# Routed experts' loop of an attention and mixture-of-experts kernel: one buffer for the next rows becomes two, each filled a step earlier

## Chip, core and metric

The kernel runs on one core of one Trainium2 chip. The metric is the device time of one execution in microseconds (us). The kernel before takes 1048.11 us, the median of 3 runs (1047.6 to 1048.34).

## What is computed

Three layers follow one another: windowed attention over 4 x 768 tokens, a dense three-way max layer, and a routed layer in which each token goes to one of 8 experts. The change touches only the last (E is 8; each expert maps 512 to 1024 and back to 512):

```python
def _moe2_ref(x, w_gate, w_output_gate, w1, w2):
    logits = x @ w_gate
    e_idx = np.argmax(logits, axis=1)
    ...
    for e in range(E):
        mask = e_idx == e
        h = np.maximum(x[mask] @ w1[e], 0.0)
        ye = h @ w2[e]
        out[mask] = gate_w[mask, None] * eom[mask, e, None] * ye
```

x has 3072 rows of 512 float32. Each float32 product is made of three products of high and low parts (`TERMS`), so one weight needs a high and a low copy.

## The kernel before

The tokens are sorted by expert into a DRAM tensor `xs`, one row of 514 values per token: 512 of x and two more, the token's id and its coefficient. After a prologue the loop at L1648 runs over steps. **A step works on two tiles of 128 rows**: tile 0 is the next 128 rows of a list that goes through the experts one after the other ("the list's rows", places in `rowi`), tile 1 the next 128 rows of the first expert ("own rows", places in `owni`). The list's expert has its 1 MB + 1 MB of weights replaced in each step, in 8 pieces of 512 KB; the first expert's weights stay.

A step, as `step` (L1443) writes it, for tile 0 and then tile 1:
- the first layer, 2 x 12 matmuls of 128x512 on TensorE (PE) at L1469, from the transposed rows `xT` of this tile, with ReLU on ScalarE (ACT) at L1475 and the transposes of its result (`h_T`, L1453) a little later;
- `ids` and `x_ids` (L1371): VectorE (DVE) copies the two extra columns of the *next* rows out of their buffer;
- `x_T` (L1355): PE transposes the *next* step's rows of this tile, four 128x128 pieces at L1362, into the PSUM bank `pTx`; ACT (L1364) and DVE (L1366, shown as L185, the line of the helper `sub`) copy the high and the low part into `xT`;
- `load` (L1349): the DMA queue SP reads a place from the list (`value_load`, L1351) and issues the 257 KB load of 128 rows of `xs` (L1353).

Then come the second layers, 2 x 24 matmuls at L1396, scaling on DVE (L1401) and a scatter of the rows by GpSimd (POOL, L1405).

The rows have one buffer, `G["xr"]`, for both tiles. `x_T(0)` reads the list's rows from it; only then can `load("owni", nxt)` refill it with the own rows that `x_T(1)` wants in the same step; after `x_T(1)`, `load("rowi", then)` refills it with the list's rows for the next step. `nxt` is i + 1, `then` is i + 2.

The order of each engine's instructions is set while the program is built: a planner (`Plan`) takes `step` and eight `split` generators, and picks what can start soonest by its own costs. A `split` (L1321) makes the high part of a weight piece on ACT and the low part on DVE, and then issues the load of that piece for the step after (L1335) on SP. So SP's order mixes the eight piece loads of a step with its two row loads, and SP takes them strictly in that order. The prologue (`pro_next`, L1552) loads three times 128 rows into three pieces of the tile `x2r`, and transposes the first two; the third piece stays as `G["xr"]`.

Of the kernel before, what the change touches and what calls it, by code (L numbers as in the profile page):

```python
# [20 lines left out]
P = 128  # L21
# [36 lines left out]
class Plan:  # L58
# [31 lines left out]
    @staticmethod  # L90
    def need(*facts):
        return ("need", facts)

    @staticmethod
    def take(tag):
        return ("take", tag)

    @staticmethod
    def op(eng, cost, r=(), w=(), tail=None, port=True):
        return ("op", eng, cost, r, w, tail, port)  # L100
# [83 lines left out]
def sub(eng, out, in0, in1):  # L184
    eng.tensor_tensor(out=out, in0=in0, in1=in1, op=ALU.subtract)  # L185
# [79 lines left out]
def local_attention_moe_kernel(  # L265
# [17 lines left out]
    nc = tc.nc  # L283
    B, H, S, HD = q.shape
    NT, D = out.shape
# [9 lines left out]
    XW = D + 2  # L295
# [6 lines left out]
    xs = dp.tile([E * REG, XW], F32, name="xs")  # L302
# [12 lines left out]
    with tc.manual_schedule(engines={mybir.EngineType.SP}):  # L315
# [3 lines left out]
        for j, src in enumerate((q, k, v)):  # L319
            t = first_t[j // 2][:, j % 2 * D : (j % 2 + 1) * D]  # L320
            first.append(t.rearrange("p (h d) -> p h d", h=H))
            nc.sync.dma_start(out=first[j], in_=src[0, :, 0:P, :].rearrange("h t d -> t h d"))
            if j:
                _, w, c = wrows[j - 1]
# [7 lines left out]
    for j in range(2):  # L332
        nc.vector.scalar_tensor_tensor(
            out=gl[:, j : j + 1], in0=nf[:, 2 * j + 1 : 2 * j + 2], scalar=4294967296.0,
# [23 lines left out]
    op, need, take, give, state = plan.op, plan.need, plan.take, plan.give, plan.state  # L358
    PE, DVE, ACT, POOL, DMA = "PE", "DVE", "ACT", "POOL", "DMA"
# [5 lines left out]
    def pe(columns, products=1):  # L365
        return products * (columns / 2400.0 + 0.013)

    def act(n):
        return 0.17 + n * 0.00085

    def dve(n):
        return 0.155 + n * 0.00104
# [4 lines left out]
    def psum(cost, r=(), w=()):  # L377

        return op(DVE, cost, r, w, port=False)

    def dma(nbytes, r=(), w=(), held=False, rate=DMA_RATE):
        return op(DMA, 0.5, r, w, tail=(0.06 + nbytes / rate, held))
# [228 lines left out]
    G = {}  # L611
# [485 lines left out]
    NL = MAXT - 2  # L1097
# [242 lines left out]
    T = {}  # L1340
    def fresh():
        ES_AT.written = LISTS_AT.written = 0.0
        for name in ("xr", "xT", "xT0", "xT1", "hr0", "hr1", "h00", "h01", "h10", "h11", "yc", "yd", "nx", "bx", "cid", "did"):
            T[name] = Buf(None)
        for name in ("pTx", "pT0", "pT1", "pH0", "pH1", "pc", "pd"):
            T[name] = Buf(None, True)
        T["W"] = [[Buf(None), Buf(None)] for _ in range(2)]

    def load(name, idx):  # L1349
        yield op(DMA, 0.6, [LISTS_AT])  # L1350
        r = nc.sync.value_load(G[name][0:1, idx], min_val=0, max_val=E * REG - P)  # L1351
        yield dma(P * XW * 4, w=[T["xr"]])
        nc.sync.dma_start(out=G["xr"], in_=xs[bass.ds(r, P), :])  # L1353

    def x_T(half):  # L1355

        xr, xb = G["xr"], T[f"xT{half}"]
        pTx = G["pTx"].rearrange("p (a b) -> p a b", b=P)
        xh, xl = [t[:, :, half * P : (half + 1) * P] for t in G["xT"]]
        for d in range(KD):  # L1360
            yield op(PE, 0.109, [T["xr"]], [T["pTx"]])
            nc.tensor.transpose(pTx[:, d, :], xr[:, d * P : (d + 1) * P], ident)  # L1362
        yield op(ACT, act(D), [T["pTx"]], [xb])
        nc.scalar.copy(out=xh, in_=pTx)  # L1364
        yield psum(dve(D), [T["pTx"], xb], [xb])
        sub(nc.vector, xl, pTx, xh.bitcast(F32))  # L1366

    def x_ids(dst):

        yield op(DVE, 0.16, [T["xr"]], [T[dst]])  # L1370
        nc.vector.tensor_copy(out=G[dst], in_=G["xr"][:, D:])  # L1371

    def ids(src, dst):
        yield op(DVE, 0.16, [T[src]], [T[dst + "id"]])
        nc.vector.tensor_copy(out=G[dst + "id"], in_=G[src][:, 0:1])
        yield op(DVE, 0.16, [T[src]], [T[dst + "id"]])
        nc.vector.tensor_copy(out=G[dst + "co"], in_=G[src][:, 1:2])
# [8 lines left out]
    def h_place(n, own, f):  # L1386

        if f == 0:
            return G["hh"][n][:, 0:4, own * P : (own + 1) * P]
        t = G["hh"][n][:, 4:6] if own else G["hx"][n]  # L1390
        return t.rearrange("p a (b c) -> p (a b) c", b=2)
# [48 lines left out]
    GROUPS = (0, 2, 3, 1)  # L1440
    FIRST_Y = (0, 1, 4, 5, 6, 7, 2, 3)

    def step(nxt, then, pl):  # L1443

        late = []

        def h_T():
            own, f = late.pop()
            hb = T[f"h{own}{f}"]
            pT = G["pg"][f].rearrange("p (a b) -> p a b", b=P)  # L1450
            for d in range(4):
                yield op(PE, 0.109, [T[f"hr{f}"]], [T[f"pT{f}"]])
                nc.tensor.transpose(pT[:, d, :], hm_t[f][:, d * P : (d + 1) * P], ident)  # L1453
            hh, hl = [h_place(m, own, f) for m in range(2)]
            yield op(ACT, act(512), [T[f"pT{f}"]], [hb])
            nc.scalar.copy(out=hh, in_=pT)
            yield psum(dve(512), [T[f"pT{f}"], hb], [hb])
            sub(nc.vector, hl, pT, hh.bitcast(F32))

        for own in range(2):  # L1460
            W, Wb = G["W"][1 - own], T["W"][1 - own]
            xT = [t[:, :, own * P : (own + 1) * P] for t in G["xT"]]
            for f in range(2):
                b = slice(f * 512, (f + 1) * 512)
                ph = G["pg"][2 + f]
                for d in range(KD):
                    yield op(PE, pe(512, 3), [T[f"xT{own}"], Wb[0]], [T[f"pH{f}"]])
                    for m, (A_, B_) in enumerate(TERMS):
                        nc.tensor.matmul(ph, lhsT=xT[A_][:, d, :], rhs=W[d][B_][:, b], start=(d + m == 0), stop=(d == KD - 1 and m == 2))  # L1469
                    if f == 1:  # L1470
                        pl.state("first", own, d)
                    if d == 2 and late:
                        yield from h_T()
                yield op(ACT, act(512), [T[f"pH{f}"]], [T[f"hr{f}"]])
                nc.scalar.activation(out=hm_t[f], in_=ph, func=AF.Relu)  # L1475
                late.append((own, f))
            yield from ids("nb"[own] + "x", "dc"[own])
            yield from x_ids("nb"[own] + "x")
            yield from x_T(own)
            yield from load(*(("rowi", then) if own else ("owni", nxt)))  # L1480
        for own in range(2):
            n = "dc"[own]
            W, Wb = G["W"][1 - own], T["W"][1 - own]
            for f in range(8):
                yield op(PE, pe(512, 3), [T[f"h{own}{f // 4}"], Wb[1]], [T["p" + n]])
                y_step(lambda m: h_place(m, own, f // 4)[:, f % 4, :], f, W, G["p" + n], f == 7)
                if f % 2:
                    pl.state("second", own, f // 2)
                if late and f == 1:
                    yield from h_T()  # L1490
            yield from y_out(n, T["p" + n], T["y" + n], T[n + "id"], True)
# [59 lines left out]

    def pro_next():  # L1552
        yield need(("lists",), ("p1",), *[("routed", n) for n in range(NTILE)])
        xbs = []
        for name, n in (("rowi", 0), ("owni", 0), ("rowi", 1)):
            xb = yield take("x2r")
            T["xr"], G["xr"] = xb, xb.t
            yield from load(name, bass.ds(n, 1))
            xbs.append(xb)
        bank = yield take("bank")  # L1560
        T["pTx"], G["pTx"] = bank, bank.t
        for t in range(2):
            T["xr"], G["xr"] = xbs[t], xbs[t].t
            yield from x_ids("nb"[t] + "x")
            T[f"xT{t}"] = T["xT"]
            yield from x_T(t)
        T["xr"], G["xr"] = xbs[2], xbs[2].t


    ET = mybir.EngineType  # L1570
# [34 lines left out]
    with tc.manual_schedule(engines={ET.PE, ET.Activation, ET.DVE, ET.Pool, ET.SP}):  # L1605
# [7 lines left out]
        for t, fill in ((rel, MASK), (rel0, 0.0)):  # L1613
            nc.gpsimd.affine_select(
                out=t, in_=rel0, pattern=[[-1, NG]], compare_op=ALU.is_ge, fill=fill, base=0, channel_multiplier=1
# [3 lines left out]
        for j in range(2):  # L1619
# [4 lines left out]
            out=reli[:, NG:], in_=reli[:, NG:], pattern=band, compare_op=ALU.is_ge, fill=MASK, base=NPREV, channel_multiplier=1  # L1624
# [21 lines left out]

    trip = nc.values_load(G["trip"][0:1, 0:1], min_val=0, max_val=NL - 2, skip_runtime_bounds_check_because="counts of tokens per expert")
    with tc.For_i(0, trip, 1, iteration_sync="reg_based") as i:  # L1648
        nxt = nc.s_assert_within(i + 1, 0, NL - 2, skip_runtime_bounds_check_because="places in the lists")
        then = nc.s_assert_within(i + 2, 0, NL - 1, skip_runtime_bounds_check_because="places in the lists")  # L1650
        fresh()
        pl = Plan(LATE_T)
        for s in staged:
            s.free = s.written = s.last = 0.0
            s.by = s.last_by = None
        pl.add(step(bass.ds(nxt, 1), bass.ds(then, 1), pl), (0,))
        for d in range(NPC):
            pl.add(split(pl, 2 * NPC + d, [("first", 0, d) if d < KD else ("second", 0, d - KD)], bass.ds(then, 1)), (2, d), HOLD_T)
        with tc.manual_schedule(engines=ALL):
            pl.run()  # L1660
# [31 lines left out]
```

## Time and profile before

| | |
|---|---|
| median of 3 runs | 1048.11 us |
| the profiled execution's own time | 1046.29 us |
| its span, first to last instruction | 1044.6 us |
| mean granted TensorE clock | 0.975 of full speed |
| PE busy | 961.0 us, 92% |
| DVE busy | 650.5 us, 62% |
| ACT busy | 498.6 us, 48% |
| POOL busy | 179.1 us, 17% |
| the loop of 13 steps, first matmul to last | 680.57 to 1035.51 us of the span, 354.94 us |

The span is the time between the first and the last instruction; 1.69 us of the profiled execution lie around it. Busy shares are of the span. The line numbers in the rows are those of the code above. A row of the timeline merges instructions of one kind: its start, its length, the engine, the line, the operation, output and input, how many, and in brackets the idle time of the engine ahead of it with what ended it.

### The profile page before, as it was taken

The numbers are of one execution on the slowest core, as the hardware profiler recorded it, in microseconds if no ns is written. First come the engines' busy times: TensorE is split into PE (matmuls) and PEld (weight loads), VectorE is DVE, ScalarE is ACT, GpSimd is POOL, SyncE is SP. The second block draws the span as 40 slices with busy tenths as digits, with TensorE's granted clock in tenths as the row PEclk, the third lists the DMA queues.
The fourth block names the chain that finished last, engine by engine and source line by source line (L and its number), as shares of the span: only waits on it lengthen the run. The fifth ranks groups of instructions, "written<-read, shape, count | busy, mean of one in ns | idle before, by whom it ended". The sixth has DMA issues, their size and how long they took to land. (4 is left out here: it accounts for less than half of the span.)

```text
span 1044.6 us, 22019 instructions
## 1 busy us (share of the span) xinstructions
PE 961.0 (92%) x7768; PEld 847.0 (81%) x7768; DVE 650.5 (62%) x1680; ACT 498.6 (48%) x1070; POOL 179.1 (17%) x246
## 2 busy tenths in 40 slices
PE   2469999999999999999999999989999999999995
PEld 2358988999989898999989998877777777777774
DVE  5998887777776667642652346655555555555553
ACT  4776665656545665422232133155554444445542
POOL 5444331213022221110110001100000000000000
PEclk9769999999999999999999999999999999999998
DMA  8998795676756677450340023376555555555555
GB/s 248 274 186 217 192 218 146 151 155 145 162 129 139 154 144 142 95 163 31 104 140 21 21 76 107 100 267 189 200 185 184 194 193 189 179 192 179 194 191 170
DMA packets 225603, 166.19 MB, mean 159 GB/s; under 512 B 181676, under 2 KB 181676, under 8 KB 225520
## 3 DMA queue, kind: packets, MB, share of 16 engines
q1 hardware_dynamic: 221360, 152.48, 54.3%
q0 software_dynamic: 4160, 12.62, 3.3%
q8 instruction: 50, 0.82, 0.3%
q14 instruction: 33, 0.27, 0.1%
HBM read 116.16 MB, written 24.78 MB: 135 GB/s over the span
## 5 line engine op out<-in xcount | busy, mean ns | idle before, releaser
L914 PE MATMUL bank<-xT,w 128*128 128x256 f32 x2592 | 336.0, 287 | 3.6 <-DVE xT L185 3.6
L914 PEld LDWEIGHTS bank<-xT,w 128*128 128x128 f32 x2592 | 318.6, 192 | 6.5 <-DVE xT L185 4.2
L185 DVE TENSOR_TENSOR w<-ws_more,w 128x1024 fp32r<-128x1024 f32 x79 | 95.5, 1222 | 71.6 <-ACT w L1321 66.0
L781 ACT ACTIVATE sp<-sp,mn 128x232 f32<-128x232 f32 (+1 forms) x192 | 90.5, 472 | 52.1 <-DVE mn L774 43.2
L986 PE MATMUL bank<-w,hh 128*128 128x512 f32 x432 | 110.4, 400 | 0.0
L944 DVE TENSOR_TENSOR hm<-hm,bank 128x512 f32<-128x512 f32 x72 | 49.3, 684 | 65.9 <-PE bank L914 64.4
L986 PEld LDWEIGHTS bank<-w,hh 128*128 128x128 f32 x432 | 77.5, 188 | 14.6
L1321 ACT CAST w<-ws_more 128x1024 fp32r<-128x1024 f32 x79 | 80.3, 1049 | 18.7 <-PE bank L1453 9.8
L1469 PE MATMUL bank<-wp,xT 128*128 128x512 f32 x312 | 82.2, 405 | 0.0
L831 PE MATMUL bank<-va,aT 128*128 128x64 bf16 x1760 | 64.8, 198 | 15.0 <-DMA aT<-nat 13.6
L1469 PE MATMUL bank<-w,xT 128*128 128x512 f32 x312 | 76.4, 394 | 1.6 <-ACTq L1648 1.6
L1475 ACT ACTIVATE hm<-bank 128x512 f32<-128x512 f32 x52 | 31.1, 597 | 95.5 <-PE bank L1469 95.5
L831 PEld LDWEIGHTS <-aT 128*128 128x128 f16 x1760 | 59.1, 101 | 20.1 <-DMA aT<-nat 15.6
L1396 PE MATMUL bank<-w,hh 128*128 128x512 f32 x246 | 68.1, 414 | 0.0
L1469 PEld LDWEIGHTS bank<-w,xT 128*128 128x128 f32 x312 | 57.6, 188 | 12.9 <-ACT xT L1364 1.8
L774 DVE CUSTOM_DVE_ANT_0 sp<-bank,bias 128x232 f32<-128x232 f32 x160 | 59.1, 389 | 10.1 <-PE bank L750 10.1
L1469 PEld LDWEIGHTS bank<-wp,xT 128*128 128x128 f32 x312 | 55.8, 189 | 10.4
L1396 PE MATMUL bank<-wp,hh 128*128 128x512 f32 x258 | 62.6, 395 | 0.0
L1086 POOL DMA_INDIRECT xs<-x2r,di x24 | 24.6, 1025 | 208.7 <-DVE x2s L185 121.4
L1396 PEld LDWEIGHTS bank<-wp,hh 128*128 128x128 f32 x258 | 48.4, 188 | 11.6
L185 POOL TENSOR_TENSOR seen<-x,dco 128x1 f32<-128x1 f32 x14 | 3.5, 252 | 303.7 <-DVE x L1401 293.6
L657 POOL TENSOR_TENSOR qkn<-qkn,va 128x512 f32<-128x512 f32 x23 | 29.3, 1272 | 139.7 <-ACT va L655 117.1
(238 smaller groups left out, 1535.3 us busy)
## 6 DMA issues: line engine op xcount, KB each, us to landing
ws_more<-in_moe_w_dram SPq DMA_DIRECT2D x85, 512.0 KB, 4.4
bias<-in_moe_w_dram SPq DMA_DIRECT2D x22, 512.0 KB, 4.6
ws<-in_moe_w_dram SPq DMA_DIRECT2D x21, 512.0 KB
x2r<-xs SPq DMA_DIRECT2D x29, 257.0 KB, 3.2
x<-xd SPq DMA_DIRECT2D x28, 256.0 KB
xd<-xo SPq DMA_DIRECT2D x24, 256.0 KB
qkn<-in_q_dram SPq DMA_DIRECT2D x23, 256.0 KB
qkn<-in_k_dram SPq DMA_DIRECT2D x23, 256.0 KB
```

What stands on the lines that cost most here:

```text
L185: eng.tensor_tensor(out=out, in0=in0, in1=in1, op=ALU.subtract)
L657: nc.gpsimd.tensor_tensor(out=vf, in0=vf, in1=va.t[:, 0, :], op=ALU.subtract)
L774: nc.vector.tensor_tensor_reduce(out=o[:, g:], in0=x[:, g:], in1=bias[:, pr, n0 + g :], scale=scale, scalar=low, op0=ALU.add, op1=ALU.min, ...
L781: nc.scalar.activation(out=o, in_=o, func=AF.Exp, scale=-1.0, bias=mn[:, h : h + 1], accum_out=sm[:, h : h + 1])
L831: nc.tensor.matmul(po[:, h, :], lhsT=a, rhs=V, start=(n == 0), stop=(n == len(terms) - 1))
L914: nc.tensor.matmul(pj[:, f2, :], lhsT=W[:, d, fs], rhs=X[:, d, :], start=(d + n == 0), stop=(d == KD - 1 and n == 2))
L944: nc.vector.tensor_max(out=hv, in0=hv, in1=pj)
L986: nc.tensor.matmul(bank.t, lhsT=X[:, f, t * P : (t + 1) * P], rhs=W[:, f, :], start=(f + n == 0), stop=(f == KF - 1 and n == 2))
L1321: (nc.scalar.copy if eng == ACT else nc.vector.tensor_copy)(out=h, in_=s.t)
L1396: nc.tensor.matmul(py, lhsT=at(A_), rhs=w, start=(f + m == 0), stop=(last and m == 2))
L1469: nc.tensor.matmul(ph, lhsT=xT[A_][:, d, :], rhs=W[d][B_][:, b], start=(d + m == 0), stop=(d == KD - 1 and m == 2))
L1475: nc.scalar.activation(out=hm_t[f], in_=ph, func=AF.Relu)
```

## The change

There are two row buffers, `G["xr"][0]` for the list's rows and `G["xr"][1]` for the own rows. In the loop each is refilled right behind the `x_T` that reads it, with the rows of the step after the next one: both loads now use `then` (i + 2). The prologue loads the first rows of both, and after each of its two `x_T` calls the rows at place 1. `x_ids` takes the tile's number, and `nxt` is gone.

```diff
--- before.py
+++ after.py
@@ -1340,35 +1340,36 @@
     T = {}
     def fresh():
         ES_AT.written = LISTS_AT.written = 0.0
-        for name in ("xr", "xT", "xT0", "xT1", "hr0", "hr1", "h00", "h01", "h10", "h11", "yc", "yd", "nx", "bx", "cid", "did"):
+        for name in ("xr0", "xr1", "xT", "xT0", "xT1", "hr0", "hr1", "h00", "h01", "h10", "h11", "yc", "yd", "nx", "bx", "cid", "did"):
             T[name] = Buf(None)
         for name in ("pTx", "pT0", "pT1", "pH0", "pH1", "pc", "pd"):
             T[name] = Buf(None, True)
         T["W"] = [[Buf(None), Buf(None)] for _ in range(2)]
 
-    def load(name, idx):
+    def load(name, idx, own):
         yield op(DMA, 0.6, [LISTS_AT])
         r = nc.sync.value_load(G[name][0:1, idx], min_val=0, max_val=E * REG - P)
-        yield dma(P * XW * 4, w=[T["xr"]])
-        nc.sync.dma_start(out=G["xr"], in_=xs[bass.ds(r, P), :])
+        yield dma(P * XW * 4, w=[T[f"xr{own}"]])
+        nc.sync.dma_start(out=G["xr"][own], in_=xs[bass.ds(r, P), :])
 
     def x_T(half):
 
-        xr, xb = G["xr"], T[f"xT{half}"]
+        xr, xb = G["xr"][half], T[f"xT{half}"]
         pTx = G["pTx"].rearrange("p (a b) -> p a b", b=P)
         xh, xl = [t[:, :, half * P : (half + 1) * P] for t in G["xT"]]
         for d in range(KD):
-            yield op(PE, 0.109, [T["xr"]], [T["pTx"]])
+            yield op(PE, 0.109, [T[f"xr{half}"]], [T["pTx"]])
             nc.tensor.transpose(pTx[:, d, :], xr[:, d * P : (d + 1) * P], ident)
         yield op(ACT, act(D), [T["pTx"]], [xb])
         nc.scalar.copy(out=xh, in_=pTx)
         yield psum(dve(D), [T["pTx"], xb], [xb])
         sub(nc.vector, xl, pTx, xh.bitcast(F32))
 
-    def x_ids(dst):
-
-        yield op(DVE, 0.16, [T["xr"]], [T[dst]])
-        nc.vector.tensor_copy(out=G[dst], in_=G["xr"][:, D:])
+    def x_ids(own):
+
+        n = "nb"[own] + "x"
+        yield op(DVE, 0.16, [T[f"xr{own}"]], [T[n]])
+        nc.vector.tensor_copy(out=G[n], in_=G["xr"][own][:, D:])
 
     def ids(src, dst):
         yield op(DVE, 0.16, [T[src]], [T[dst + "id"]])
@@ -1440,7 +1441,7 @@
     GROUPS = (0, 2, 3, 1)
     FIRST_Y = (0, 1, 4, 5, 6, 7, 2, 3)
 
-    def step(nxt, then, pl):
+    def step(then, pl):
 
         late = []
 
@@ -1475,9 +1476,9 @@
                 nc.scalar.activation(out=hm_t[f], in_=ph, func=AF.Relu)
                 late.append((own, f))
             yield from ids("nb"[own] + "x", "dc"[own])
-            yield from x_ids("nb"[own] + "x")
+            yield from x_ids(own)
             yield from x_T(own)
-            yield from load(*(("rowi", then) if own else ("owni", nxt)))
+            yield from load(("rowi", "owni")[own], then, own)
         for own in range(2):
             n = "dc"[own]
             W, Wb = G["W"][1 - own], T["W"][1 - own]
@@ -1551,20 +1552,18 @@
 
     def pro_next():
         yield need(("lists",), ("p1",), *[("routed", n) for n in range(NTILE)])
-        xbs = []
-        for name, n in (("rowi", 0), ("owni", 0), ("rowi", 1)):
-            xb = yield take("x2r")
-            T["xr"], G["xr"] = xb, xb.t
-            yield from load(name, bass.ds(n, 1))
-            xbs.append(xb)
+        G["xr"] = []
+        for own in range(2):
+            T[f"xr{own}"] = xb = yield take("x2r")
+            G["xr"].append(xb.t)
+            yield from load(("rowi", "owni")[own], bass.ds(0, 1), own)
         bank = yield take("bank")
         T["pTx"], G["pTx"] = bank, bank.t
-        for t in range(2):
-            T["xr"], G["xr"] = xbs[t], xbs[t].t
-            yield from x_ids("nb"[t] + "x")
-            T[f"xT{t}"] = T["xT"]
-            yield from x_T(t)
-        T["xr"], G["xr"] = xbs[2], xbs[2].t
+        for own in range(2):
+            T[f"xT{own}"] = T["xT"]
+            yield from x_ids(own)
+            yield from x_T(own)
+            yield from load(("rowi", "owni")[own], bass.ds(1, 1), own)
 
 
     ET = mybir.EngineType
@@ -1646,14 +1645,13 @@
 
     trip = nc.values_load(G["trip"][0:1, 0:1], min_val=0, max_val=NL - 2, skip_runtime_bounds_check_because="counts of tokens per expert")
     with tc.For_i(0, trip, 1, iteration_sync="reg_based") as i:
-        nxt = nc.s_assert_within(i + 1, 0, NL - 2, skip_runtime_bounds_check_because="places in the lists")
         then = nc.s_assert_within(i + 2, 0, NL - 1, skip_runtime_bounds_check_because="places in the lists")
         fresh()
         pl = Plan(LATE_T)
         for s in staged:
             s.free = s.written = s.last = 0.0
             s.by = s.last_by = None
-        pl.add(step(bass.ds(nxt, 1), bass.ds(then, 1), pl), (0,))
+        pl.add(step(bass.ds(then, 1), pl), (0,))
         for d in range(NPC):
             pl.add(split(pl, 2 * NPC + d, [("first", 0, d) if d < KD else ("second", 0, d - KD)], bass.ds(then, 1)), (2, d), HOLD_T)
         with tc.manual_schedule(engines=ALL):
```

What the planner makes of it on the engines follows at three places. `L1351 TENSOR_LOAD` is the reading of the place, `L1353 DMA x2r<-xs` the load of 128 rows, `L1335 DMA` and `L1308 DMA` loads of weight pieces (in the loop and in the prologue), `ISA` and `REGISTER_ALU` bookkeeping. A wait in brackets names the semaphore: an engine's, or that of a DMA slot (`DMAHW0` to `DMAHW7`, given to the DMAs of the loop's body in turn, so the fourth DMA has `DMAHW3`, the sixth `DMAHW5`); the ending `_own` marks those that the loop's body counts, the others are from the prologue.

SP in the loop, from behind the third piece load of a step, before:

```order
L1351 TENSOR_LOAD owni
L1351 ISA x2
L1353 ISA
L1353 DMA x2r<-xs 128x514 [waits DMAHW5_I-9128_own,DMAHW3_I-9128_own,PE_I-9128_own]
L1335 ISA
L1335 DMA ws_more<-in_moe_w_dram 128x1024 [waits DVE_I-9128_own,DMAHW4_I-9128_own,Activation_I-9128_own,DMAHW4_49]
L1351 ISA
L1351 TENSOR_LOAD rowi
L1351 ISA x2
L1353 ISA
L1353 DMA x2r<-xs 128x514 [waits DMAHW3_I-9128_own,DVE_I-9128_own,PE_I-9128_own]
```

and now:

```order
L1351 TENSOR_LOAD rowi
L1351 ISA x2
L1353 ISA
L1353 DMA x2r<-xs 128x514 [waits DMAHW3_I-9138_own,PE_I-9138_own,DMAHW4_49]
L1335 ISA
L1335 DMA ws_more<-in_moe_w_dram 128x1024 [waits DVE_I-9138_own,DMAHW4_I-9138_own,Activation_I-9138_own,DMAHW3_49]
L1351 ISA
L1351 TENSOR_LOAD owni
L1351 ISA x2
L1353 ISA
L1353 DMA x2r<-xs 128x514 [waits DVE_I-9138_own,DMAHW5_I-9138_own,PE_I-9138_own,DMAHW7_49]
```

The places of the two row loads among the piece loads are the same. The fourth DMA of the body was the own rows' load and is now the list rows', the sixth the other way round.

PE in the loop, around `x_T(1)` at the end of the first layers, before:

```order
L1453 MATMUL bank_525<-ident,hm_546 128x128 [waits DVE_I-9128_own,Activation_I-9128_own]
L1453 MATMUL bank_525<-ident,hm_546 128x128 x3
L1469 MATMUL bank_530<-wp_6756,xT_717 128x512 x2
L1469 MATMUL bank_530<-wp_6756,xT_718 128x512
L1362 REGISTER_ALU
L1362 MATMUL bank_524<-ident,x2r 128x128 [waits DMAHW3_I-9128_own,DVE_I-9128_own]
L1362 MATMUL bank_524<-ident,x2r 128x128 x3
L1396 MATMUL bank_527<-w_676,hh_1869 128x512
```

and now:

```order
L1454 MATMUL bank_525<-ident,hm_546 128x128 [waits DVE_I-9138_own,Activation_I-9138_own]
L1454 MATMUL bank_525<-ident,hm_546 128x128 x3
L1470 MATMUL bank_530<-wp_6756,xT_717 128x512 x2
L1470 MATMUL bank_530<-wp_6756,xT_718 128x512
L1362 REGISTER_ALU
L1362 MATMUL bank_524<-ident,x2r 128x128 [waits DMAHW5_I-9138_own,DVE_I-9138_own,DMAHW7_49]
L1362 MATMUL bank_524<-ident,x2r 128x128 x3
L1397 MATMUL bank_527<-w_676,hh_1869 128x512
```

The order is the same. The transposes waited for the fourth DMA of the body, which SP issues ahead of them in the same step; now they wait for the sixth, which SP issues behind them, so it is the one of the step before.

SP in the prologue, before (a piece load follows at once, eight in a row):

```order
L1351 TENSOR_LOAD owni [waits DVE_49]
L1351 ISA x2
L1353 ISA
L1353 DMA x2r<-xs 128x514 [waits DVE_49,DMASW1_49,PE_49,DMASW7_49,Activation_49,Pool_49]
L1351 TENSOR_LOAD rowi
L1351 ISA x2
L1353 ISA
L1353 DMA x2r<-xs 128x514 [waits DVE_49,DMASW2_49,PE_49,DMASW5_49,Activation_49,Pool_49]
L1305 TENSOR_LOAD esi [waits DVE_49]
L1305 ISA x2
L1308 ISA
L1308 DMA ws_more<-in_moe_w_dram 128x1024
```

and now, behind the first four piece loads:

```order
L1351 TENSOR_LOAD rowi
L1351 ISA x2
L1353 ISA
L1353 DMA x2r<-xs 128x514 [waits DMAHW4_49,DMAHW6_49,DVE_49,PE_49]
L1308 ISA
L1308 DMA ws_more<-in_moe_w_dram 128x2x512 [waits DMAHW5_49]
L1308 ISA
L1308 DMA ws_6757<-in_moe_w_dram 128x2x512 [waits Activation_49]
L1351 TENSOR_LOAD owni
L1351 ISA x2
L1353 ISA
L1353 DMA x2r<-xs 128x514 [waits DMAHW7_49,DVE_49,PE_49]
```

One row load that stood ahead of all eight piece loads now stands behind four of them, and another that was the first step's stands behind six; each waits for PE and DVE to have read the buffer.

## Rows read from the trace of the kernel before

**Rows 1.** Chain of work that ended last, shares of the span by line.

```profile
PE bank L1396 14%; PE bank L1469 11%; DMA x2r<-xs 5%; PE bank L1453 2%; PE bank L1362 1%; POOLq L1687 0%; DVE x L1401 0%; POOL seen L185 0%; POOLq L1648 0%; POOLq L1405 0%; POOLq L185 0%
```

**Rows 2.** Waits of PE in the loop: us in total, times, longest us.

```profile
PE bank L1362 <- DMA x2r<-xs: 23.7, 13, 2.5
```

**Rows 3.** Timeline of PE, third step, around `x_T(0)` and `x_T(1)`.

```profile
739.44 0.94 PE L1469 MATMUL bank<-w,xT 128*128 128x512 f32 x3
740.23 0.60 PE L1362 MATMUL bank<-ident,x2r 128*128 128x128 f32 x4
740.58 2.35 PE L1469 MATMUL bank<-wp,xT 128*128 128x512 f32 x9
...
746.53 0.94 PE L1469 MATMUL bank<-wp,xT 128*128 128x512 f32 x3
748.98 0.63 PE L1362 MATMUL bank<-ident,x2r 128*128 128x128 f32 x4 [1.50 <-DMA x2r<-xs]
749.36 1.64 PE L1396 MATMUL bank<-w,hh 128*128 128x512 f32 x6
750.84 0.60 PE L1453 MATMUL bank<-ident,hm 128*128 128x128 f32 x4
```

**Rows 4.** Timeline of the other engines, third step.

```profile
743.63 0.68 DVE L185 TENSOR_TENSOR xT<-bank,xT 128x512 fp32r<-128x512 f32 x1
745.09 0.33 SPq L1353 DMA_DIRECT2D x2r<-xs  x1
747.57 0.60 ACT L1475 ACTIVATE hm<-bank 128x512 f32<-128x512 f32 x1 [0.17 <-PE bank L1469]
748.10 0.14 DVE L1377 COPY cco<-bx 128x1 f32<-128x1 f32 x1
758.19 0.37 SPq L1335 DMA_DIRECT2D ws_more<-in_moe_w_dram  x1
```

**Rows 5.** Steps: us, busy of PE, PEld, DVE, ACT, POOL (instructions), PEclk, DMA share, GB/s.

```profile
680.57:707.46 26.89, 25.46 (x121) 20.50 (x122) 14.56 (x21) 13.59 (x18) 1.20 (x2) 1.00 0.78 269
734.48:761.20 26.72, 25.22 (x122) 20.23 (x121) 15.32 (x22) 13.59 (x18) 2.37 (x4) 1.00 0.58 199
815.97:845.24 29.27, 26.80 (x121) 21.43 (x121) 15.40 (x22) 13.59 (x18) 2.38 (x4) 0.94 0.53 166
872.00:900.95 28.95, 26.79 (x121) 21.43 (x121) 15.40 (x22) 13.58 (x18) 2.38 (x4) 0.94 0.54 176
```

**Rows 6.** Timeline of PE, the longest waits of `x_T(1)`: fifth, sixth, eighth step.

```profile
803.75 0.63 PE L1362 MATMUL bank<-ident,x2r 128*128 128x128 f32 x4 [2.49 <-DMA x2r<-xs]
831.43 0.63 PE L1362 MATMUL bank<-ident,x2r 128*128 128x128 f32 x4 [2.47 <-DMA x2r<-xs]
887.16 0.90 PE L1362 MATMUL bank<-ident,x2r 128*128 128x128 f32 x4 [2.16 <-DMA x2r<-xs]
```

**Rows 7.** Short windows behind these waits and a long one earlier, columns as in rows 5.

```profile
803.00:805.00 2.00, 1.25 (x8) 1.14 (x9) 0.17 (x1) 0.54 (x1) 0.00 (x0) 1.00 0.24 95
833.00:835.00 2.00, 2.00 (x8) 1.63 (x7) 0.52 (x1) 0.89 (x1) 0.00 (x0) 0.50 0.51 132
889.00:891.00 2.00, 2.00 (x9) 1.51 (x8) 0.52 (x1) 0.21 (x1) 0.00 (x0) 0.55 0.43 132
180.00:320.00 140.00, 140.00 (x1642) 129.11 (x1641) 104.46 (x353) 81.60 (x238) 29.07 (x36) 1.00 0.69 147
```

**Rows 8.** Loads of rows in the loop: us from issue to landing.

```profile
DMA to landing us min/median/max: 2.6/3.2/4.7
```

**Rows 9.** Timeline of the prologue's end and the first step: SP, DVE and PE.

```profile
669.75 2.99 SPq L1353 DMA_DIRECT2D x2r<-xs  x3
673.54 2.99 SPq L1308 DMA_DIRECT2D ws_more<-in_moe_w_dram  x5
677.23 0.16 DVE L1371 COPY nx<-x2r 128x2 f32<-128x2 f32 x1
686.57 0.60 PE L1362 MATMUL bank<-ident,x2r 128*128 128x128 f32 x4
```

## The prediction

> **What bounds the kernel now.** I read the chain of waits first [rows 1]: what ended last is work of PE, with one other entry of weight, the row loads x2r<-xs, at 5% of the span (some 52 us). That is more than a change of the load can win, since the chain counts each load from its issue, while PE still works for most of it. The waits of PE in the loop say what it really costs [rows 2]: from the first step's start to the last one's end PE waits for one thing only, 13 times, once a step, for 23.7 us in all, and it is the transposes of x_T at L1362.
>
> The timeline of the third step shows which of the two x_T it is [rows 3]. x_T(0) starts right behind three matmuls, without a wait. x_T(1) ends a wait of 1.50 us. The engine rows beside it show why [rows 4]: the own rows' load is issued at 745.09, because the one buffer had to be read by x_T(0) first and because SP was still at the weight pieces; PE is done with its first layer near 747.4; the load takes 2.6 to 4.7 us to land [rows 8].
>
> The table of steps says that nothing else holds PE there [rows 5]: the third step lasts 26.72 us with PE busy for 25.22, and the difference is just the 1.50 us of the wait. ACT with 13.59 and DVE with 15.32 are far from the step's length, the DMA share is near 0.6. So each step is PE's work plus one load that comes too late.
>
> **The change part by part.** *The wait of x_T(1) goes*: x_T(1) now waits for a load that was issued a step earlier. In the loop the own rows' load is issued once x_T(1) and the copy bx are through. That copy stands on DVE behind the one that starts at 748.10 [rows 4], so the issue comes near 749; the rows are wanted a step of some 25 us later, near 772. The landing takes 4.7 us at most [rows 8], so about 18 us of cover are left. The list rows' load, issued near 745 as the own rows' was, is wanted by the next step's x_T(0), some 20 us later. Gain: 13 waits, 23.7 us [rows 2].
>
> *PE's pipeline closes over the gap.* From the start of the three matmuls ahead of it to the start of the matmuls behind it, x_T(0) takes 740.58 - 739.44 = 1.14 us, x_T(1) takes 749.36 - 746.53 = 2.83 us [rows 3]. The difference is 1.69 us, and the wait is 1.50 of it; the other 0.19 us is the end of one group that otherwise overlaps the next. 13 x 0.19 = 2.5 us, so 26.2 us with the waits.
>
> *The clock.* Two steps, the sixth and the eighth, are longer than their wait explains: 29.27 - 2.47 = 26.80 and 28.95 - 2.16 = 26.79 us, against 26.72 - 1.50 = 25.22 [rows 3, 5, 6]. In both the granted clock is 0.50 to 0.55, so the lower of the two levels, 1.2 GHz, in a window right behind the wait, and PE had just stood idle for over 2 us; the fifth step's 2.49 us wait is followed by full clock [rows 6, 7]. Each fall costs 1.58 us, two of them 3.15. Without idle time in the step I take them as gone, since earlier PE is busy without a break for 140 us at a clock of 1.00 [rows 7]. Sum: 26.2 + 3.15 = 29.35 us.
>
> The Trainium skill bears on this in "TensorE: Matmul & The Clock Gate", Part 1: the gate follows PE's activity in a free-running window that does not start with the work, so that it is a matter of phase which gap costs. That agrees with a fall behind 2.16 us and none behind 2.49; it would also make the number of falls differ from run to run, and one more fall in the runs than in the profiled execution would be 1.58 of the 1.82 us between them. By that, all falls gone, the median would end near the profiled sum. The same page, under "HAM oscillation", gives as its abstract rule that only longer idle gaps than these reopen the throttle; by that rule the two falls have some other cause and stay. That is a rival below.
>
> *What takes the wait's place in a step.* With x_T(1) 1.69 us earlier, three things stand next. The bank pTx is free when DVE ends the low part of x_T(0), 743.63 + 0.68 = 744.31, 3 us ahead of x_T(1). The rows have landed. The last h_T of the step, at 750.84 now, will want to start at 749.15, and needs ACT's ReLU at 747.57 + 0.60 = 748.17 [rows 3, 4]: 0.98 us of slack. All other work of ACT and DVE in the second layers starts from PE's matmuls and moves with them. The weight pieces are loaded a step ahead: the last is issued at 758.19 [rows 4] and split a step later, so a step that is 2 us shorter leaves over 15 us of cover. Cost 0.
>
> *SP in the loop* has the same order; only the names of the two row loads are exchanged. The first still stands behind the third piece load and needs x_T(0); the second still needs x_T(1). Cost 0.
>
> *The prologue* trades one row load ahead of the eight piece loads for two among them. The first of these must wait for the copy nx, 677.23 + 0.16 = 677.39, and its rows are wanted at 686.57 [rows 9]. It has four piece loads of 512 KB ahead of it. The three row loads of before start 1.33 us apart (2.99 us for three, less one's own 0.33, over two), so without the third the pieces start near 673.54 - 1.33 = 672.2; 2.1 MB and 0.26 MB at the 269 GB/s of the first step [rows 5] take 8.8 us, so landing is near 682 and, by the longest landing after issue, 677.4 + 4.7 = 682.1: 4 us of cover. At worst it shares the DMA engines with all eight pieces and both row loads, 4.7 MB in 17.5 us, and lands at 689.7: 3.1 us late, once. Bounds 0 and 3.1; I take 0, as the loads start in order. The loop's first load of SP comes at some 682, and the first row it has to serve is a step away. The extra rows of DVE and SP are single register instructions: 0.
>
> **The sum.** The profiled execution took 1046.29 us, 1.82 less than the median of the runs. 1046.29 - 29.35 = 1016.9. From the median, 1048.11 - 29.35 = 1018.8, and a third fall that goes too would make it 1017.2. I take **1017.5 us**, nearer the sum that counts a third fall.
>
> **The rivals.**
> - *The falls of the clock stay* (the rule named above, as a mechanism: something other than the idle time lowers it for some 3 us, twice or three times in the loop). Then only the 26.2 us come: 1046.29 - 26.2 = 1020.1, from the median 1021.9. For it: 2.49 us of idle time without a fall. Against it: both falls begin right behind a wait, and among the longest three [rows 6, 7]. Chance 0.08.
> - *ACT takes the wait's place*: the last h_T of each step waits for ReLU, which has only 0.98 us of slack. If ACT runs another 0.6 us copy ahead of it and PE arrives earlier than I think, 0.5 us stay in each step: 13 x 0.5 = 6.5, so 1024.0. Against it: the ReLU stands ahead of that copy on ACT now. Chance 0.05.
> - *The change does not do what it says*: both buffers are pieces of one tile, and a wait on the whole tile would tie x_T(1) to the load of this step, issued even later. Then 1048. Against it: the wait names the sixth DMA alone. Chance 0.02.
> - *Slower, by the clock*: 325 us of PE work without a pause could lower the granted clock for long stretches. At half clock each us gives half a us of work, so the loss passes the gain of 29.35 us from 59 us at half clock on; 100 us at it would give 1017.5 + 50 = 1067.5. Against it: 140 us of PE without a pause at 1.00 [rows 7]. Chance 0.02.
>
> **How the numbers follow.** The forecast has 0.83. The range goes from 1014 (some 3 us below the lowest sum, for a pipeline gain of 0.4 instead of 0.19 us a step) to 1022.5 (the clock's rival from the median, or the prologue's 3.1 us on the higher sum); it leaves out the last three rivals, 0.09. A measurement can tell about 0.2%, 2.1 us, from no change. Faster: forecast, clock's rival and ACT's rival, 0.96. Same: 0.02. Slower: 0.02.
>
> **What would show it.** In the profile after: no wait of L1362 for x2r<-xs in the loop, each x_T(1) some 0.8 us behind the start of the three matmuls ahead of it, steps of 25.0 us each with granted clock 1.00, and a loop of about 325.6 us (354.94 in the table of the profile before, less 29.35). PE's busy time would fall by 3 us at most. Wrong would be a step with full clock above 25.3 us (then a new wait stands in it, and its releaser names the rival), steps with a clock of 0.94, or a first step that stands out by a wait of x_T(0) (the prologue's loads).

## The result and the profile after

The changed kernel takes **1017.0 us** (median of 4 runs, 1016.35 to 1018.69) against 1048.05 us of the kernel before (4 runs). The ratio is 0.9707, 95% interval 0.969 to 0.9723. The profiled execution took 1016.92 us, 29.37 less than that of before.

The head of the page and its chain of work that ended last (by engine, by line):

```profile
span 1015.4 us, 22036 instructions
PE 955.8 (94%) x7768; PEld 845.3 (83%) x7768; DVE 651.2 (64%) x1680; ACT 497.0 (49%) x1070; POOL 178.8 (18%) x246
...
PE 32%; POOLq 0%; issue 0%; DVE 0%; POOL 0%
PE bank L1470 14%; PE bank L1397 14%; PE bank L1454 2%; PE bank L1362 1%; POOLq L1685 0%; DVE x L1402 0%; POOL seen L185 0%; POOLq L1647 0%; POOLq L1406 0%; POOLq L185 0%
```

The row loads have left the chain [rows 1]. (Most lines of the step have moved down by one, so the first layer is L1470 and the second L1397; x_T is still L1362.) The waits of PE from the second transposes of the prologue to the last step (us in total, times, longest us):

```profile
PE bank L1470 <- ACTq L1647: 1.5, 1, 1.5
PE bank L1362 <- DVE xT L185: 1.4, 1, 1.4
```

Both stand before the first matmul of the loop. The 13 waits for x2r<-xs [rows 2] are gone, and none has come in their place. The third step on PE, with the same pieces as [rows 3]:

```profile
736.21 0.94 PE L1470 MATMUL bank<-w,xT 128*128 128x512 f32 x3
736.99 0.60 PE L1362 MATMUL bank<-ident,x2r 128*128 128x128 f32 x4
737.34 2.35 PE L1470 MATMUL bank<-wp,xT 128*128 128x512 f32 x9
...
743.30 0.94 PE L1470 MATMUL bank<-wp,xT 128*128 128x512 f32 x3
744.07 0.60 PE L1362 MATMUL bank<-ident,x2r 128*128 128x128 f32 x4
744.43 1.63 PE L1397 MATMUL bank<-w,hh 128*128 128x512 f32 x6
745.90 0.60 PE L1454 MATMUL bank<-ident,hm 128*128 128x128 f32 x4
```

From the three matmuls ahead of x_T(1) to the matmuls behind it now takes 744.43 - 743.30 = 1.13 us, as for x_T(0); it was 2.83 [rows 3]. SP issues the two row loads of the same step at these times:

```profile
741.86 0.33 SPq L1353 DMA_DIRECT2D x2r<-xs  x1
...
745.48 0.33 SPq L1353 DMA_DIRECT2D x2r<-xs  x1
```

The first is the list rows' load, wanted by the next step's x_T(0) at 761.99; the second the own rows', wanted at 769.08. They land as slowly as before, which no longer matters:

```profile
DMA to landing us min/median/max: 2.8/3.7/4.8
```

The steps (us, busy time and number of instructions of PE, PEld, DVE, ACT, POOL, granted clock, DMA share, GB/s):

```profile
679.28:706.08 26.80, 26.80 (x120) 21.55 (x121) 14.57 (x21) 13.48 (x18) 2.21 (x3) 0.94 0.81 269
706.08:731.09 25.01, 25.01 (x122) 20.28 (x120) 15.33 (x22) 13.48 (x18) 2.39 (x4) 1.00 0.65 209
...
981.15:1006.16 25.01, 25.01 (x121) 20.10 (x119) 15.32 (x22) 13.48 (x18) 2.38 (x4) 1.00 0.64 206
sum 326.88, PE 326.88 PEld 264.81 DVE 198.45 ACT 175.27 POOL 30.82; mean PE 25.14 PEld 20.37 DVE 15.27 ACT 13.48 POOL 2.37
```

and the last matmuls of the loop:

```profile
1004.79 1.53 PE L1397 MATMUL bank<-w,hh 128*128 128x512 f32 x6
```

Twelve of the 13 steps take 25.00 or 25.01 us at full clock, and PE is busy for all of it. From the first matmul to the end of the last, as in the table of the kernel before, the loop takes 1004.79 + 1.53 - 679.28 = 327.04 us (the sum of the rows stops 0.16 us ahead of that end), against 354.94: 27.90 less. It also begins 1.29 us earlier, 679.28 against 680.57; the loads ahead of it already went out 1.19 us earlier (668.56 against 669.75 [rows 9]), so that came from the work before the changed code. It differs between executions: in the changed kernel's second profile, shown below, the loop begins at 680.73. What follows the loop takes 9.1 us, as before. 27.90 + 1.29 = 29.2 us of span.

### The profile page after: what moved, and what is told of

It reads as the page before. It is cut to its first block, busy times and chain, and to the rows that moved or that the text cites. A ratio compares the mean times of both kernels' runs of the same rounds, so it can differ in the third digit from the quotient of the medians.

```text
span 1015.4 us, 22036 instructions
## 1 busy us (share of the span) xinstructions
PE 955.8 (94%) x7768; PEld 845.3 (83%) x7768; DVE 651.2 (64%) x1680; ACT 497.0 (49%) x1070; POOL 178.8 (18%) x246
## 5 line engine op out<-in xcount | busy, mean ns | idle before, releaser
L986 PE MATMUL bank<-w,hh 128*128 128x512 f32 x432 | 110.4, 400 | 0.0
L1470 PE MATMUL bank<-wp,xT 128*128 128x512 f32 x312 | 82.1, 405 | 0.0
L1470 PE MATMUL bank<-w,xT 128*128 128x512 f32 x312 | 78.1, 400 | 1.5 <-ACTq L1647 1.5
L1470 PEld LDWEIGHTS bank<-w,xT 128*128 128x128 f32 x312 | 58.7, 192 | 13.4 <-ACT xT L1364 1.7
L1397 PE MATMUL bank<-w,hh 128*128 128x512 f32 x246 | 65.5, 401 | 0.0
L1470 PEld LDWEIGHTS bank<-wp,xT 128*128 128x128 f32 x312 | 55.7, 189 | 10.5
L1397 PE MATMUL bank<-wp,hh 128*128 128x512 f32 x258 | 62.6, 395 | 0.0
L1397 PEld LDWEIGHTS bank<-wp,hh 128*128 128x128 f32 x258 | 48.4, 188 | 11.6
L185 DVE TENSOR_TENSOR nat<-sp,nat 128x928 f16<-128x928 f32 (+1 forms) x45 | 52.0, 1155 | 1.1 <-ACT nat L795 0.3
```

Of the source, the lines that this page charges most:

```text
L986: nc.tensor.matmul(bank.t, lhsT=X[:, f, t * P : (t + 1) * P], rhs=W[:, f, :], start=(f + n == 0), stop=(f == KF - 1 and n == 2))
L1397: nc.tensor.matmul(py, lhsT=at(A_), rhs=w, start=(f + m == 0), stop=(last and m == 2))
```

## The experiments

The theory: each step lost the time by which the own rows landed after PE wanted them, and now and then a fall of TensorE's clock behind that idle time. Three questions were open: whether the buffer or the time of issue did it, whether the clock really falls because of the wait, and what holds the kernel now. The first three runs shared one chip, on which the kernel before took 1043.32 us (13 runs, 1037.62 to 1050.51); the last three shared another, with 1047.74 us (9 runs, 1043.06 to 1048.97).

### The second buffer alone

From the changed kernel, with the loads at their old places (the rows of places i + 1 and i + 2, as before):

```diff
-            yield from load(("rowi", "owni")[own], then, own)
+            yield from load(*(("rowi", then, 0) if own else ("owni", nxt, 1)))
```

The step takes `nxt` (i + 1) again for this. In the prologue only the list's rows are loaded a second time.

> Two row buffers, but both loads at their old places: the own rows' load still fetches the next step's rows, and the planner still puts it behind the third piece load of the step. My theory: SP's order, not the buffer, set when the own rows' load went out (x_T(0) is through 4 us before it). So the load goes out as late as before, x_T(1) waits 1.4 to 2.5 us in each of 13 steps, some 23.7 us in all, and the time is that of the kernel before: 1046 to 1049.5 us. Rival: the buffer held the load back; then it goes out 2 us or more earlier, the waits fall below 0.5 us, and the time is 1017 to 1024 us.

Measured: 1048.27 us (10 runs, 1044.38 to 1051.21), ratio to the kernel before 1.0031 (1.0003 to 1.0059). Waits of PE in the loop, then SP and PE in the third step, and that step (columns as above):

```profile
PE bank L1362 <- DMA x2r<-xs: 22.6, 13, 2.7
PE bank L1362 <- issue: 1.7, 1, 1.7
```

```profile
742.75 3.80 SPq L1335 DMA_DIRECT2D ws_more<-in_moe_w_dram  x3
747.55 0.33 SPq L1353 DMA_DIRECT2D x2r<-xs  x1
```

```profile
742.61 0.60 PE L1362 MATMUL bank<-ident,x2r 128*128 128x128 f32 x4
...
752.55 1.09 PE L1362 MATMUL bank<-ident,x2r 128*128 128x128 f32 x4 [2.69 <-DMA x2r<-xs]
```

```profile
736.71:767.44 30.73, 28.04 (x122) 22.46 (x121) 15.40 (x22) 13.59 (x18) 2.38 (x4) 0.89 0.49 170
```

The buffer of the own rows had been free for most of a step, and still the load went out at 747.55, 4.3 us after x_T(0) was through, right behind the third piece load. That piece load waits for VectorE's low part of the piece, and SP waits with it, as the waits of SP in the loop of this run say:

```profile
SPq L1335 <- DVE w L185: 221.5, 88, 8.8
```

So a second buffer by itself gives nothing: the planner's place of the load in SP's order set the time. Whether the 0.3% by which it came out slower is real stays open; the runs of both kernels scatter by 7 to 13 us on this chip. Part of it may be the wait of 1.7 us, which x_T(0) has in the first step and which the kernel before has not. The profile names no releaser for it. The row load that this x_T(0) reads went out at 679.77, behind the eight piece loads of the prologue, and ahead of them before [rows 9], so it is the likely cause. The clock fell in 3 of the 13 steps, behind waits of 2.69, 2.42 and 2.42 us; the profiled execution was the slowest of the ten (1051.21 us).

### One buffer, with the load issued earlier

From the kernel before; the first three piece loads of a step wait, in the plan, until the own rows' load has its place on SP (the upper lines are in `step`, the lower ones in `split`):

```diff
             yield from load(*(("rowi", then) if own else ("owni", nxt)))
+            if not own:
+                pl.state("ownload")
...
         if then:
+            if d < 3:
+                yield need(("ownload",))
             if d == 0:
```

> One row buffer as before, but the own rows' load goes ahead of the first three piece loads of the step on SP. It still has to wait for x_T(0) and for the copy nx, which ends near 742.45 in the third step of the kernel before, where the load went out at 745.09. My theory: what cost the time was when the load went out; some 2.5 us earlier it lands about when x_T(1) wants it. Waits of 0 to 0.3 us a step (0 to 4 us in all), no fall of the clock in the loop: 1017 to 1022 us, and the piece loads that go out 2 us later cost nothing. Rival: a whole step of lead is needed, because the landing varies between 2.6 and 4.7 us; then waits of 0.5 us and more stay, 1024 to 1032 us.

Measured: 1019.39 us (4 runs, 1017.01 to 1019.63), ratio 0.9746 (0.9699 to 0.9793). SP and PE in the third step, the steps (columns as above) and the landing:

```profile
741.54 0.35 SPq L1354 DMA_DIRECT2D x2r<-xs  x1
742.85 2.24 SPq L1336 DMA_DIRECT2D ws_more<-in_moe_w_dram  x4
```

```profile
745.48 0.94 PE L1470 MATMUL bank<-wp,xT 128*128 128x512 f32 x3
746.26 0.60 PE L1363 MATMUL bank<-ident,x2r 128*128 128x128 f32 x4
746.61 1.63 PE L1397 MATMUL bank<-w,hh 128*128 128x512 f32 x6
```

```profile
683.17:708.27 25.10, 25.10 (x121) 20.38 (x121) 14.57 (x21) 13.49 (x18) 1.25 (x3) 1.00 0.80 282
708.27:733.27 25.00, 25.00 (x121) 20.30 (x120) 15.33 (x22) 13.48 (x18) 2.39 (x4) 1.00 0.58 210
```

```profile
DMA to landing us min/median/max: 4.0/4.4/5.4
```

The load goes out 2.4 us after x_T(0)'s transposes start (739.17), where it took 4.9 us before [rows 3, 4], and x_T(1) follows 4.7 us later without a wait. The steps are those of the changed kernel, 25.0 us, with one buffer and all piece loads behind the row load. So neither the second buffer nor a whole step of lead is needed for the gain; some 2.5 us of earlier issue are. The cover is thin, though: 4.7 us from issue to use against landings of 4.0 to 5.4 (over both loads of a step). The changed kernel has over 20 us between them.

### The load issued later

From the kernel before, the own rows' load one place later, behind the fourth piece load:

```diff
+            if not own:
+                yield need(("issued", 2 * NPC + 3))
             yield from load(*(("rowi", then) if own else ("owni", nxt)))
```

> One row buffer as before, with the own rows' load one place later on SP, behind the fourth piece load: the wait of x_T(1) becomes longer by some 2 us, so 3.3 to 4.5 us a step, 25 us more in all. My theory: the clock falls because PE stands idle, so it now falls in most steps, each fall costing 1.6 us or more: PE busy above 26 us in most steps, granted clock 0.90 to 0.95 there, time 1082 to 1097 us. Rival: the falls have another cause; then two or three steps show one as before, and the time is 1070 to 1076 us.

Measured: 1081.03 us (4 runs, 1077.49 to 1081.28), ratio 1.0331 (1.028 to 1.0382). Waits of PE in the loop; four of the waits; and steps 1, 2, 6 and 8 (columns as above):

```profile
PE bank L1362 <- DMA x2r<-xs: 45.6, 13, 3.7
```

```profile
696.79 0.63 PE L1362 MATMUL bank<-ident,x2r 128*128 128x128 f32 x4 [3.45 <-DMA x2r<-xs]
725.61 0.80 PE L1362 MATMUL bank<-ident,x2r 128*128 128x128 f32 x4 [3.61 <-DMA x2r<-xs]
847.14 1.09 PE L1362 MATMUL bank<-ident,x2r 128*128 128x128 f32 x4 [3.67 <-DMA x2r<-xs]
908.48 0.63 PE L1362 MATMUL bank<-ident,x2r 128*128 128x128 f32 x4 [3.43 <-DMA x2r<-xs]
```

```profile
680.05:708.84 28.79, 25.33 (x120) 20.30 (x121) 14.57 (x21) 13.60 (x18) 1.20 (x2) 1.00 0.73 251
708.84:739.24 30.40, 26.79 (x121) 21.44 (x120) 15.40 (x22) 13.59 (x18) 2.38 (x4) 0.94 0.52 176
830.32:861.59 31.27, 27.60 (x121) 22.14 (x120) 15.40 (x22) 13.59 (x18) 2.39 (x4) 0.89 0.50 163
891.90:920.54 28.64, 25.21 (x122) 20.22 (x120) 15.32 (x22) 13.59 (x18) 2.39 (x4) 1.00 0.52 180
```

The waits are twice as long in sum, and the clock falls in 10 of 13 steps (all but the first, eighth and twelfth) where it fell in 2 of 13 before and in 3 of 13 with the buffer alone on this chip. A step with a fall keeps PE busy for 26.79 to 26.81 us instead of 25.21, so 1.6 us each, and 2.4 in the sixth step. The falls come with the idle time, so the rival that gives them another cause has fallen. The sum closes: 13 x 25.21 = 327.7, and 45.6 of waits, and 10 falls with some 16.7 (nine of 1.59 and one of 2.39), make 390.0 us; from the loop's first matmul at 680.05 to the end of its last six (1068.86 + 1.53) it took 390.3. The time is 1 us below the range given, since the waits were 3.2 to 3.7 us and not up to 4.5, and three steps kept their clock.

### The changed kernel again, two banks in the prologue, and the early load again

> The changed kernel itself, unedited, as a control beside the others of this call. My theory: PE no longer waits for any load in the loop, so its time does not hang on how fast loads land: 1015.5 to 1019 us, whatever the kernel before takes on this chip and however its runs spread. Rival: the time follows the chip, and moves with the kernel before by several us.

Measured: 1018.22 us (5 runs, 1016.63 to 1019.24), ratio 0.9724 (0.9701 to 0.9747). That is inside the range given, but it does not decide between the theory and its rival: the kernel before took nearly the same beside both sets of runs, 1048.05 and 1047.74 us.

The changed kernel, with a bank of its own for each x_T of the prologue:

```diff
-        bank = yield take("bank")
-        T["pTx"], G["pTx"] = bank, bank.t
         for own in range(2):
+            bank = yield take("bank")
+            T["pTx"], G["pTx"] = bank, bank.t
             T[f"xT{own}"] = T["xT"]
```

> The changed kernel, with a PSUM bank of its own for each of the two x_T calls of the prologue, so that the second does not wait for VectorE to empty the bank of the first (1.40 us of PE in the changed kernel's profile), and the loop begins some 1.2 us earlier. My theory: the prologue's end is on the path, as the loop behind it is nothing but PE: 1.2 us less than the changed kernel in the same call, and up to 1.8 us more where the first step's fall of the clock goes too: 1013 to 1017 us. Rival: the loop's entry is held by something else (the wait at its first matmul only grows by what the other loses): the same time as the changed kernel.

Measured: 1017.3 us (5 runs, 1014.55 to 1017.68), ratio 0.9711 (0.9687 to 0.9735). PE from the prologue's transposes to the second step, first in the changed kernel on this chip (and there the loop's last matmuls too), then with two banks:

```profile
676.63 0.60 PE L1362 MATMUL bank<-ident,x2r 128*128 128x128 f32 x4
678.63 0.66 PE L1362 MATMUL bank<-ident,x2r 128*128 128x128 f32 x4 [1.40 <-DVE xT L185]
680.73 5.12 PE L1470 MATMUL bank<-w,xT 128*128 128x512 f32 x21 [1.44 <-ACTq L1647]
...
705.94 4.92 PE L1470 MATMUL bank<-w,xT 128*128 128x512 f32 x21
...
1004.78 1.53 PE L1397 MATMUL bank<-w,hh 128*128 128x512 f32 x6
```

```profile
676.61 1.04 PE L1362 MATMUL bank<-ident,x2r 128*128 128x128 f32 x8
678.65 0.47 PE L1470 MATMUL bank<-w,xT 128*128 128x512 f32 x1 [1.00 <-ACTq L1647]
...
704.34 4.92 PE L1470 MATMUL bank<-w,xT 128*128 128x512 f32 x21
```

The transposes start together and the second step begins 705.94 - 704.34 = 1.60 us earlier: the prologue's end is on the path, and the trace gives this version about the gain that was expected. The medians differ by 0.9 us, and the intervals of the ratios overlap, so the runs don't show it; the median is 0.3 us above the range given.

> One row buffer, own rows' load ahead of the step's first three piece loads, once more, beside the changed kernel on the same chip. My theory: equal to the changed kernel within 2 us, since both have steps of 25.0 us. Rival: where loads land later its smaller cover runs out, and waits of a few tenths of a us a step make it 3 us or more slower than the changed kernel.

Measured: 1017.61 us (5 runs, 1016.55 to 1019.52), ratio 0.9723 (0.9699 to 0.9746). Beside the changed kernel's 0.9724 it is the same. In its profile PE waits for no row load in the loop, so the thin cover held in this execution too.

## Why the prediction was right

1017.5 us was forecast, 1017.0 measured, inside 1014 to 1022.5. By its own steps:

- **The wait of x_T(1) goes, 23.7 us.** Right: no wait for a row load is left. The reason named, one buffer that x_T(0) had to free first, was only half of it. It stood beside the other half, SP being at the weight pieces, and the run with the buffer alone shows that SP's order decided: the load went out no earlier with its buffer free.
- **PE's pipeline closes over the gap, 0.19 us a step.** Right: 1.13 us around x_T(1) against the 1.14 taken from x_T(0).
- **The clock, 3.15 us.** The cause is shown by the later load (10 falls with longer waits), and the size holds for most falls, 1.6 us each against 1.58. Two cost more: 2.39 us in the sixth step of the later load, and 2.84 (28.04 against 25.20) in the third step with the buffer alone. In the changed kernel no fall is left behind an x_T in the loop. But the premise that all are gone was too much for this one execution, and a step with a clock of 0.94 was one of the prediction's own signs of being wrong: the first step of the loop runs at 0.94 and lasts 26.80 us, 1.6 more than the 25.21 of the changed kernel's second profile (705.94 - 680.73). This fall stands behind the two short idle times of PE in the prologue, 1.40 and 1.47 us, which were there before the change too (1.40 and 1.55 us, without a fall). Of the two profiles of the changed kernel one has it, and of the profiles with the early load or two banks none.
- **What takes the wait's place: nothing.** Right. The last h_T, with 0.98 us of slack, starts 1.47 us after the matmuls ahead of it, as it did before (750.84 - 749.36 = 1.48 [rows 3]).
- **SP in the loop and in the prologue, 0.** Right: x_T(0) of the first step has no wait. Only the time given for SP's first load in the loop, some 682, was wrong: it went out at 686.81 before and goes out at 687.10 now.

Forecast for the loop were 325.6 us. It took 327.04. The changed kernel's second profile, without a fall in the loop, took 1004.78 + 1.53 - 680.73 = 325.58, so there the terms come out as forecast. That the loop began 1.29 us earlier in this profile made up for most of that fall, by chance. One of the signs was wrong, too: PE's busy time was to fall by 3 us at most, and it fell by 5.2, from 961.0 to 955.8. The profile counts PE as busy in the 0.19 us a step and in the falls of the clock (25.22 us in the third step before, 25.00 now), so these terms of the prediction's own sum, 2.5 and 3.15 us, should have stood in that sign. Of the rivals, the one that keeps the falls is refuted, ACT's wait did not come, and the two others did not happen. The doubt about which sum to start from, 1016.9 or 1018.8, lay within the scatter: the changed kernel itself gave medians of 1017.0 and 1018.22 in its two sets of runs. That the runs of the kernel before had a third fall, which drew the forecast down to 1017.5, is not shown: one execution of it was profiled. How near the forecast came is in that part luck.

One figure in the description of the kernel before was wrong, and no step used it: eight pieces of 512 KB make 4 MB per expert, 2 MB for each of its two matrices.

## What to carry to other kernels

When an engine waits for a load, ask first what held its issue: here not the buffer but the in-order queue, whose instruction ahead was waiting for VectorE. Moving the load up by 2.5 us on that queue gave the whole gain without a second buffer; the second buffer, with the load a step ahead, gives the same time with 20 us from issue to use instead of 4.7. A wait on a busy TensorE costs more than its length: read what the pieces around it take without a wait, and the granted clock behind it.

## What the runs showed of the hardware

The granted clock fell to its lower level behind idle times of 2.16 and 2.47 us and not behind 2.49 us in one execution; in another, with waits of 3.17 to 3.67 us, it fell in 10 steps, and not behind waits of 3.43, 3.45 and 3.45 us. So which wait costs the extra 1.6 us can't be read from its length in this range. Behind the 20 shorter waits of x_T(1), 0.51 to 1.86 us, in the kernel before and in the run with the buffer alone, it did not fall. Where the four transposes behind a wait themselves took 1.09 us instead of some 0.63, the clock was low already when PE went on, and those two falls cost more than the others, 2.84 and 2.39 us. The Trainium skill, "TensorE: Matmul & The Clock Gate", Part 1, says that the gate's window runs free of the work; these rows agree, with a fall behind 2.16 us and none behind 2.49. The Trainium skill's section "HAM oscillation" on the same page gives a rule by which gaps as short as 2.16 us would do nothing; the rows disagree with it, and the rows decide.

The kernel before spread over 13 us from run to run on one chip (1037.62 to 1050.51), and the changed kernel over 2.6 us on another where the kernel before spread over 5.9. What the waits do from run to run wasn't profiled for the kernel before on those chips; that they carry the spread is likely, and not shown.
